# Loading K transposed by DMA in a two-layer decode attention kernel

## Chip, cores and metric

The kernel runs on one core of a Trainium2 chip. The metric is the device time of one execution, in microseconds, and a kernel's time is the median of its runs. The profile used for the reading is that of one more execution of the same program.

## What is computed

Eight batch elements with one token each go through the same attention block and the same small MLP twice. There are 32 query heads, 8 key/value heads (four query heads share one), 8192 cached keys, and heads of 128 elements. Everything in memory is bf16. Both layers read the same K and V caches, which hold 134 MB each.

```python
def _A_ref(x, k_cache, v_cache, wq, wo):
    q = (x @ wq).reshape(B, Sq, Hq, Dh).transpose(0, 2, 1, 3)     # Sq = 1
    k = jnp.repeat(k_cache, rep, axis=1)                         # [B, 8, 8192, 128] -> 32 heads
    v = jnp.repeat(v_cache, rep, axis=1)
    scores = jnp.einsum("bhqd,bhkd->bhqk", q, k) * (Dh ** -0.5)
    p = _softmax(scores, axis=-1)
    o = jnp.einsum("bhqk,bhkd->bhqd", p, v)
    return o.transpose(0, 2, 1, 3).reshape(B, Sq, Hq * Dh) @ wo
...
x = x + _A_ref(_layernorm(x), A_k_cache, A_v_cache, A_wq, A_wo)
x = x + silu(_layernorm(x) @ w1) @ w2
x = x + _A_ref(_layernorm(x), A_k_cache, A_v_cache, A_wq, A_wo)
x = x + silu(_layernorm(x) @ w1) @ w2
```

## The kernel before

**Tasks and steps.** A task is one layer, one batch element and one key/value head: 128 tasks. Its 8192 keys are four granules of 2048 keys, and a granule is two steps of 1024 keys, so a task has eight steps (`GPT`) and the program 1024 positions. `make_tasks` writes the order of tasks out by hand, so that the second layer of one batch element lies among the first layer of the next.

**Loads.** A granule of K or of V is half a megabyte and fills one slot of an arena in SBUF with 27 slots. `plan_loads` works out ahead of time which load goes into which slot and after which position of the program it may be issued. The last 18 granules of K of a batch element (`KEEP`) stay in their slots, transposed, from the first layer to the second. So there are 512 loads of V and 368 of K. All loads are issued by SyncE (SP) into one queue, through `issue` and `dma` (L311), and a load that is to overwrite a slot first waits for the last reader of that slot. A partition p of a slot receives the 16 consecutive rows p*16 to p*16+15 of the granule, 4 KB in one run, so column block c of a slot holds the keys p*16 + c.

**A step.** At position p the loop at the end issues, in this order: the transposes of K for position p + 3 (`emit_t`, `LT` = 3), the scores of position p (`emit_s`), the PV product of position p - 14 (`emit_pv`, `LP` = 14), one piece of the softmax, and, when one is pending, one stage of the chain that follows attention.

- `emit_t` (L408) makes eight PE transposes of 128x128 into a bank of PSUM, and a copy brings the bank back into the same slot: on ScalarE (L414) for three of eight, on VectorE (L416) for the others. It is left out for granules that are kept.
- `emit_s` (L443) makes two matmuls, each with 512 keys as the moving operand. The query stands in a zeroed 128-column window that is shifted by one column for each block of 512 keys, so that 16 blocks and 4 heads fill 64 rows of one PSUM bank.
- The softmax takes a maximum (L452 to L462), an exponential on ScalarE (L466), a sum (L472, L475), and four PE transposes of the probabilities (L484) whose copy is `PT` (L488).
- `emit_pv` (L505) makes eight matmuls: the stationary operand is a 128x128 block of V, and the moving one the four columns of probabilities of that block's keys. These columns lie 16 elements apart in `PT`.
- `emit_norm` (L519) multiplies the four output columns by the reciprocal of the sum.

**The chain.** When a batch element's last first-layer task is done, `chain_of` queues its output projection, layer norm, MLP, second layer norm and second query projection (the matmuls are at L573). One stage is taken at each position, and each stands in PE's program order between the steps of attention, so PE waits there for VectorE's layer norm. The same block for all eight batch elements at once ends the program.

Every engine executes in program order. Waits are semaphore waits that `Sync` derives from who wrote and read each named buffer.

Of the kernel before, what the change touches and what calls it, by code (L numbers as in the profile page):

```python
# [12 lines left out]
GRP = 8  # L13
GPT = 8
GPG = 2
# [8 lines left out]
NQB = 2  # L24
NST = 4
KB = 512
ACT_EVAC = (1, 4, 7)

BF16 = mybir.dt.bfloat16
# [3 lines left out]
ALU = mybir.AluOpType  # L33
# [3 lines left out]
class Tok:  # L37
    __slots__ = ("sem", "val")

    def __init__(self, sem, val):  # L40
        self.sem = sem
        self.val = val
# [78 lines left out]
class Load:  # L121
# [4 lines left out]
    def __init__(self, kind, b, g, k, need, free):  # L126
        self.kind, self.b, self.g, self.k = kind, b, g, k
        self.need, self.free = need, free
        self.slot, self.after = None, None


def make_tasks(nb, nkv, keep_from):
# [57 lines left out]
def _build(ctx, nc, A_x, A_k_cache, A_v_cache, A_wq, A_wo, B_w1, B_w2, out):  # L190
# [4 lines left out]
    REP = HQ // HKV  # L195
# [3 lines left out]
    NGRAN = NCH // (GRP * GPG)  # L199
    SLOT = GRP * GPG * 128  # L200
# [3 lines left out]
    kept = set(order[len(order) - KEEP:])  # L204
# [7 lines left out]
    dve = nc.vector  # L212
    act = nc.scalar
    pool = nc.gpsimd
    sp = nc.sync
# [3 lines left out]
    def sb(shape, dt, name):  # L219
        _cnt[0] += 1  # L220
        return ctx.enter_context(nc.sbuf_tensor(f"{name}_{_cnt[0]}", shape, dt))

    def ps_bank(name, dt=FP32):
        _cnt[0] += 1
        n = 512 if dt == FP32 else 1024
        return ctx.enter_context(nc.psum_tensor(f"{name}_{_cnt[0]}", [128, n], dt))

    ARENA = sb([128, NSLOT * SLOT], BF16, "arena")

    def chunk(slot, c):  # L230
        o = slot * SLOT + c * 128
        return ARENA[:, o:o + 128]

    def half(slot, h):
        o = slot * SLOT + h * GRP * 128
        return ARENA[:, o:o + GRP * 128]
# [6 lines left out]
    XT = [sb([128, KT, B], BF16, f"XT{n}") for n in range(3)]  # L243
    NJ = NCH * 128 // KB
    NR = NJ * REP
    CPB = KB // 128
    JPG = GRP * 128 // KB
    assert NR <= 128 and NJ % 16 == 0 and JPG * KB == GRP * 128
    QT1 = sb([128, B * HQ], BF16, "QT1")
    QT2 = [sb([128, HQ], BF16, "QT2") for _ in range(2)]  # L250
    QB = [sb([128, NJ - 1 + 128], BF16, "QB") for _ in range(NQB)]
# [11 lines left out]
    hsT = sb([128, FT * B], BF16, "hsT")  # L263
    assert KB == D
    P = sb([128, KB], BF16, "P")
    Xr = P
# [8 lines left out]
    rcp = [sb([128, REP], FP32, "rcp") for _ in range(NST)]  # L275

    SCp = [ps_bank("SCp") for _ in range(NSCP)]
    OTp = [ps_bank("OTp") for _ in range(2)]
# [4 lines left out]
    slsem = [DmaCounter(syn.new_sem(f"sl{i}")) for i in range(NSLOT)]  # L283
# [5 lines left out]
    def res(name):  # L289
        if name not in R:  # L290
            R[name] = Res(name)
        return R[name]

    def r_half(slot, h):
        return res(f"slot{slot}_{h}")

    def op(eng, inst_fn, reads=(), writes=()):
        reads = [res(n) if isinstance(n, str) else n for n in reads]
        writes = [res(n) if isinstance(n, str) else n for n in writes]
        syn.acquire(eng, reads, writes)  # L300
        inst = inst_fn()
        tok = syn.mark(inst, eng)
        syn.release(tok, reads, writes)
        return tok

    def dma(eng, out_ap, in_ap, counter, reads=(), writes=()):
        reads = [res(n) if isinstance(n, str) else n for n in reads]
        writes = [res(n) if isinstance(n, str) else n for n in writes]
        syn.acquire(eng, reads, writes)
        tok = counter.next_tok()  # L310
        eng.dma_start(out_ap, in_ap).then_inc(counter.sem, 16)  # L311
        syn.release(tok, reads, writes)
        return tok

    def mm_group(steps, reads=(), writes=()):
        def run():
            inst = None
            for f in steps:
                inst = f()
            return inst  # L320
        return op(pe, run, reads, writes)
# [6 lines left out]

    def issue(d):
        cache = A_k_cache if d.kind == "K" else A_v_cache  # L330
        src = cache[d.b, d.g].rearrange("(k p c) d -> k p (c d)", k=NGRAN, p=128)[d.k]
        dst = ARENA[:, d.slot * SLOT:(d.slot + 1) * SLOT]
        dma(sp, dst, src, slsem[d.slot], writes=[r_half(d.slot, 0), r_half(d.slot, 1)])
        (k_slot if d.kind == "K" else v_slot)[(d.b, d.g, d.k)] = d.slot

    with nc.Block() as block:

        @block.sync
        def _(sync_eng):
            dma(sp, Xr[0:B, :], x_in, wsem["x"], writes=["P"])  # L340

            op(pool, lambda: pool.memset(ident[:, :], 1.0), writes=["ident"])
# [6 lines left out]
                reads=["ident"], writes=["ident"],  # L349
# [5 lines left out]
            for n in range(NST):  # L355
# [5 lines left out]
                reads=["ident"], writes=["hm"],  # L361
# [4 lines left out]
            def issue_until(pos):  # L366
                while queue and queue[0].after <= pos:
                    issue(queue.pop(0))

            def load_wq():  # L370
                src = A_wq.rearrange("(kt p) n -> p kt n", p=128)
                h = KT // 2
                dma(sp, wq_sb[:, 0:h, :], src[:, 0:h, :], wsem["wq"], writes=["wq"])
                dma(sp, wq_sb[:, h:KT, :], src[:, h:KT, :], wsem["wq"], writes=["wq"])
# [6 lines left out]
            for _n in range(NGRAN):  # L381
                issue(queue.pop(0))
# [7 lines left out]

            def has_t(i):
                layer, _b, g = tasks[i // GPT]
                return layer == 0 or (g, (i % GPT) // GPG) not in kept

            def where(i):
                _l, b, g = tasks[i // GPT]
                return b, g, (i % GPT) // GPG, i % GPG

            def emit_t(i):
# [12 lines left out]
                dst = half(slot, h)  # L412
                if n % 8 in ACT_EVAC:
                    op(act, lambda: act.copy(dst, TPp[tb][:, :]), reads=[f"TP{tb}"], writes=[r_half(slot, h)])  # L414
# [3 lines left out]
            def emit_t_until(i):  # L418
                while tnext[0] <= min(i, NG - 1):
                    if has_t(tnext[0]):  # L420
                        emit_t(tnext[0])
                    tnext[0] += 1
# [10 lines left out]
            def emit_s(i):  # L433
                ti = i // GPT
                b, g, k, h = where(i)
                slot = k_slot[(b, g, k)]
                bank, qn = ti % NSCP, ti % NQB
                keys = half(slot, h)
                steps = []
                for c in range(JPG):  # L440
                    j = (i % GPT) * JPG + c
                    steps.append(
                        lambda c=c, j=j: pe.matmul(  # L443
                            SCp[bank][:, :], QB[qn][:, NJ - 1 - j:NJ - 1 - j + 128], keys[:, c * KB:(c + 1) * KB],
                            start=(j == 0), stop=(j == NJ - 1),
                        )
                    )
                mm_group(steps, reads=[r_half(slot, h), f"QB{qn}"], writes=[f"SC{bank}"])
# [45 lines left out]
            def emit_pv(i):  # L494
                ti = i // GPT
                b, g, k, h = where(i)
                slot = v_slot[(b, g, k)]
                ob, pb = ti % 2, ti % NPT
                pv = PT[pb][:, :, :].rearrange("p c (r j) -> p c j r", j=NJ)
                otp = OTp[ob][:, 0:REP]  # L500
                steps = []
                for c in range(GRP):
                    cc = (i % GPT) * GRP + c
                    steps.append(
                        lambda c=c, cc=cc: pe.matmul(  # L505
                            otp, chunk(slot, h * GRP + c), pv[:, cc % CPB, cc // CPB, :],
                            start=(cc == 0), stop=(cc == NCH - 1),
                        )
                    )
                mm_group(steps, reads=[r_half(slot, h), f"PT{pb}"], writes=[f"OT{ob}"])  # L510

            def emit_norm(ti):
                layer, b, g = tasks[ti]
                ob, st = ti % 2, ti % NST
                if layer == 0:
                    dst, rd = at1[b % 2][:, g * REP:(g + 1) * REP], f"at1_{b % 2}"
                else:
                    dst, rd = at2[:, g * REP:(g + 1) * REP, b], "at2"
                op(dve, lambda: dve.tensor_tensor(dst, OTp[ob][:, 0:REP], rcp[st][:, :], ALU.mult),  # L519
                   reads=[f"OT{ob}", f"rcp{st}"], writes=[rd])  # L520

            def ln_stages(xv, rx, n):
# [100 lines left out]
            def chain_of(b):  # L623
# [16 lines left out]
                reads=["P", "ident"], writes=["MISC"],  # L640
            )
            op(dve, lambda: dve.tensor_copy(XT[0][:, :, :], MISC[:, 0:KT * B].rearrange("p (k b) -> p k b", b=B)),
               reads=["MISC"], writes=["XT0"])
# [13 lines left out]
            for p in range(NG + LP + GPT + 1):  # L657
                tq = (p + LQ) // GPT
                if (p + LQ) % GPT == 0 and tq < ntask:
                    layer, b, _g = tasks[tq]  # L660
# [15 lines left out]
                if done >= 0 and done % GPT == 0 and done // GPT < ntask:  # L676
                    tj = done // GPT
                    emit_norm(tj)
                    layer, b, _g = tasks[tj]
# [7 lines left out]
            for f in block_stages(  # L687
# [11 lines left out]
                reads=["XT0", "ident"], writes=["MISC"],  # L699
# [33 lines left out]
```

## Time and profile before

| | |
|---|---|
| Median of 3 runs | 1338.75 us (1329.92 to 1340.53) |
| Profiled execution: time, span | 1341.24 us, 1339.1 us |
| Granted TensorE clock, mean | 0.928 |
| Busy: PE, DVE, ACT, POOL | 1177.7 us (88%), 632.0 us (47%), 391.9 us (29%), 70.9 us (5%) |
| Read from memory | 473.44 MB, 354 GB/s over the span |
| K loads, V loads | 368 and 512, 512 KB each; median 12.8 and 10.1 us from issue to landing |

The span is what the profile's instructions cover; the time has a little around it. Busy time of PE is not PE at its peak, since matmuls overlap: the durations in the timeline overlap too, and what an instruction really occupies is read from start to start. The DMA share in a stretch is the mean busy share of the core's 16 DMA engines; around 1 they are full. The granted clock is given as a share of full speed.

### The profile page before, as it was taken

The numbers are of one execution on the slowest core, as the hardware profiler recorded it, in microseconds if no ns is written. First come the engines' busy times: TensorE is split into PE (matmuls) and PEld (weight loads), VectorE is DVE, ScalarE is ACT, GpSimd is POOL, SyncE is SP. The second block draws the span as 40 slices with busy tenths as digits, with TensorE's granted clock in tenths as the row PEclk, the third lists the DMA queues.
The fourth block names the chain that finished last, engine by engine and source line by source line (L and its number), as shares of the span: only waits on it lengthen the run. The fifth ranks groups of instructions, "written<-read, shape, count | busy, mean of one in ns | idle before, by whom it ended". The sixth has DMA issues, their size and how long they took to land.

```text
span 1339.1 us, 45854 instructions
## 1 busy us (share of the span) xinstructions
PE 1177.7 (88%) x19644; PEld 909.4 (68%) x19960; DVE 632.0 (47%) x1977; ACT 391.9 (29%) x670; POOL 70.9 (5%) x176
## 2 busy tenths in 40 slices
PE   3978799889988899889998889988998889988896
PEld 3656667676767667677676766767776776767665
DVE  2544345544554445545455444554545445445443
ACT  1323123323233223322233222432323222333220
POOL 0000000000000000000000000000000000000000
PEclk7989799989999799998999789997999979999796
DMA  8999599979999699987999779997999959999693
GB/s 348 385 400 405 200 391 407 387 261 399 408 409 357 234 392 408 407 340 275 410 408 405 284 297 402 407 403 272 377 408 407 383 191 383 408 408 372 229 409 154
DMA packets 133944, 476.45 MB, mean 356 GB/s; under 512 B 14176, under 2 KB 20080, under 8 KB 133232
## 3 DMA queue, kind: packets, MB, share of 16 engines
q1 hardware_dynamic: 133744, 473.51, 90.6%
q8 instruction: 159, 2.61, 0.8%
q14 instruction: 41, 0.34, 0.1%
HBM read 473.44 MB, written 0.01 MB: 354 GB/s over the span
## 4 chain that ended last, share of the span: by engine, by line
PE 45%; DMA 41%; DVE 6%; SPq 3%; issue 3%; POOL 0%; ACT 0%; POOLq 0%; DVEq 0%
DMA arena<-in_A_k_cache_dram 40%; PE SCp L443 18%; PE TPp L408 11%; PE OTp L505 8%; PE MISC L573 7%; SPq L311 3%; PE TPp L484 1%; DVE arena L416 1%; DMA wq<-in_A_wq_dram 1%; DVE yr L559 1%; DVE tr L557 1%; DVE tr L556 1%; DVE mxa L452 1%; DVE xnT L561 0%; DVE yr L551 0%
## 5 line engine op out<-in xcount | busy, mean ns | idle before, releaser
L443 PE MATMUL SCp<-arena,QB 128*128 128x512 bf16 x1732 | 561.9, 392 | 24.5 <-PE TPp L408 3.1
L505 PEld LDWEIGHTS OTp<-PT,arena 128*128 128x128 bf16 x8192 | 365.4, 97 | 265.6 <-issue 26.9
L408 PE MATMUL TPp<-ident,arena 128*128 128x128 bf16 x5888 | 474.7, 227 | 72.1 <-DMA arena<-in_A_k_cache_dram 59.8
L416 DVE COPY arena<-TPp 128x1024 bf16<-128x1024 bf16 x460 | 318.1, 692 | 387.1 <-PE TPp L408 386.7
L414 ACT COPY arena<-TPp 128x1024 bf16<-128x1024 bf16 x276 | 279.3, 1012 | 677.6 <-PE TPp L408 677.6
L408 PEld LDWEIGHTS TPp<-ident,arena 128*128 128x128 bf16 x5888 | 356.7, 101 | 98.2 <-DMA arena<-in_A_k_cache_dram 82.6
L505 PE MATMUL OTp<-PT,arena 128*128 128x4 bf16 x8192 | 365.5, 169 | 9.6 <-DMA arena<-in_A_v_cache_dram 8.0
L443 PEld LDWEIGHTS SCp<-arena,QB 128*128 128x128 bf16 x2048 | 153.3, 101 | 7.6 <-PE SCp L443 5.3
L466 ACT ACTIVATE P<-SCp,mxb 64x512 bf16<-64x512 f32 x128 | 87.3, 682 | 178.3 <-DVE mxb L462 175.0
L475 POOL PARTITION_ALL_REDUCE ssa<-ssm x128 | 55.5, 434 | 1065.6 <-DVE ssm L472 1065.6
L452 DVE TENSOR_REDUCE mxa<-SCp 64x1 f32<-64x512 f32 x128 | 85.6, 669 | 29.5 <-PE SCp L443 29.5
L488 DVE COPY PT<-TPp 128x256 bf16<-128x256 bf16 x128 | 37.4, 292 | 109.8 <-PE TPp L484 109.8
L573 PE MATMUL MISC<-xnT,wq 128*128 128x1 bf16 (+1 forms) x1152 | 31.6, 165 | 29.9 <-DVE xnT L561 29.9
L573 PEld LDWEIGHTS MISC<-xnT,wq 128*128 128x128 bf16 x1152 | 30.9, 102 | 30.6 <-DVE xnT L561 25.6
L484 PE MATMUL TPp<-ident,P 128*128 128x128 bf16 x512 | 49.9, 220 | 0.0
L472 DVE TENSOR_SCALAR ssm<-hm,rs 64x4 f32<-64x4 f32 x128 | 27.6, 215 | 36.4 <-ACT P L466 36.4
L431 ACT COPY QB<-QT 128x4 bf16<-128x4 bf16 x128 | 26.2, 206 | 32.6 <-DVE QT L619 32.6
L573 PE MATMUL MISC<-at,wo 128*128 128x1 bf16 (+1 forms) x1152 | 30.9, 164 | 3.5 <-issue 3.2
L573 PEld LDWEIGHTS MISC<-at,wo 128*128 128x128 bf16 x1152 | 30.1, 97 | 3.8 <-issue 3.4
L484 PEld LDWEIGHTS TPp<-ident,P 128*128 128x128 bf16 x512 | 30.3, 97 | 0.3
L519 DVE TENSOR_TENSOR at<-OTp,rcp 128x4 bf16<-128x4 f32 x128 | 21.1, 165 | 15.0 <-PE OTp L505 15.0
L462 DVE STREAM_TRANSPOSE mxb<-mxa 64x32 f32<-64x32 f32 x128 | 26.1, 204 | 4.4
(46 smaller groups left out, 254.9 us busy)
## 6 DMA issues: line engine op xcount, KB each, us to landing
arena<-in_A_v_cache_dram SPq DMA_DIRECT2D x512, 512.0 KB, 10.1
arena<-in_A_k_cache_dram SPq DMA_DIRECT2D x368, 512.0 KB, 12.8
wq<-in_A_wq_dram SPq DMA_DIRECT2D x2, 2048.0 KB, 9.0
wo<-in_A_wo_dram SPq DMA_DIRECT2D x1, 4096.0 KB, 26.1
w<-in_B_w_dram SPq DMA_DIRECT2D x2, 1792.0 KB, 22.6
P<-in_A_x_dram SPq DMA_DIRECT2D x1, 8.0 KB
out_dram<-P SPq DMA_DIRECT2D x1, 8.0 KB
```

Source lines behind the costliest of these rows:

```text
L311: eng.dma_start(out_ap, in_ap).then_inc(counter.sem, 16)
L408: lambda c=c: pe.transpose(tpv[:, c, :], chunk(slot, h * GRP + c), ident[:, :])
L414: op(act, lambda: act.copy(dst, TPp[tb][:, :]), reads=[f"TP{tb}"], writes=[r_half(slot, h)])
L416: op(dve, lambda: dve.tensor_copy(dst, TPp[tb][:, :]), reads=[f"TP{tb}"], writes=[r_half(slot, h)])
L443: lambda c=c, j=j: pe.matmul(SCp[bank][:, :], QB[qn][:, NJ - 1 - j:NJ - 1 - j + 128], keys[:, c * KB:(c + 1) * KB], start=(j == 0), stop=( ...
L452: op(dve, lambda: dve.tensor_reduce(mxa[:, 0:1], SCp[bank][0:NR, :], AX.X, ALU.max), reads=[f"SC{bank}"], writes=["mxa"])
L466: op(act, lambda: act.activation(P[0:NR, :], SCp[bank][0:NR, :], ACT.Exp, bias=mxb[:, 0:1], scale=SM_SCALE, accum_out=rs[st][:, :]), reads ...
L475: op(pool, lambda: pool.partition_all_reduce(ssa[st][:, :], ssm[st][:, :], 128, bass.bass_isa.ReduceOp.add), reads=[f"ssm{st}"], writes=[f ...
L484: lambda c=c: pe.transpose(tpv[:, c, :], P[:, c * 128:(c + 1) * 128], ident[:, :])
L488: op(dve, lambda: dve.tensor_copy(PT[pb][:, :, :], tpv[:, :, 0:NR]), reads=[f"TP{tb}"], writes=[f"PT{pb}"])
L505: lambda c=c, cc=cc: pe.matmul(otp, chunk(slot, h * GRP + c), pv[:, cc % CPB, cc // CPB, :], start=(cc == 0), stop=(cc == NCH - 1),)
L573: lambda o=o, k=k: pe.matmul(MISC[:, o * n:(o + 1) * n], w_sb[:, k, o * 128:(o + 1) * 128], rhs_of(k), start=(k == 0), stop=(k == kparts - 1),
```

## The change

`by_dma` decides which granules of K are loaded by a DMA that transposes; it returns True for all. Such a load writes the 128 elements of a head to the 128 partitions and the granule's 2048 keys, in their order in memory, along a partition. `has_t` is then never true, so `emit_t` issues nothing: 5888 transposes on PE and 736 copies are gone. Since V's rows are still spread as before, the scores of a block must come out in the order of V's blocks: the moving operand of a scores matmul is now four runs of 128 keys, each run stepping through the slot sixteen elements at a time. In PV each of the four moving columns is given eight times (`PVN`), so that a matmul has 32 moving columns and writes 32 columns of PSUM; `emit_norm` reads every eighth. The plan of loads, the slots, and the order on SP stay as they were.

```diff
+PVN = 8
...
+def by_dma(g, k):
+    return True
...
-    def dma(eng, out_ap, in_ap, counter, reads=(), writes=()):
+    def dma(eng, out_ap, in_ap, counter, reads=(), writes=(), turn=False):
...
-        eng.dma_start(out_ap, in_ap).then_inc(counter.sem, 16)
+        if turn:
+            eng.dma_start_transpose(out_ap, in_ap).then_inc(counter.sem, 16)
+        else:
+            eng.dma_start(out_ap, in_ap).then_inc(counter.sem, 16)
...
-        src = cache[d.b, d.g].rearrange("(k p c) d -> k p (c d)", k=NGRAN, p=128)[d.k]
         dst = ARENA[:, d.slot * SLOT:(d.slot + 1) * SLOT]
-        dma(sp, dst, src, slsem[d.slot], writes=[r_half(d.slot, 0), r_half(d.slot, 1)])
+        if d.kind == "K" and by_dma(d.g, d.k):
+            src = cache[d.b, d.g].rearrange("(k n) d -> k n d", k=NGRAN)[d.k]
+            dst = dst.rearrange("p (o n) -> p o n", o=1)
+        else:
+            src = cache[d.b, d.g].rearrange("(k p c) d -> k p (c d)", k=NGRAN, p=128)[d.k]
+        dma(sp, dst, src, slsem[d.slot], writes=[r_half(d.slot, 0), r_half(d.slot, 1)],
+            turn=d.kind == "K" and by_dma(d.g, d.k))
...
             def has_t(i):
                 layer, _b, g = tasks[i // GPT]
-                return layer == 0 or (g, (i % GPT) // GPG) not in kept
+                k = (i % GPT) // GPG
+                return not by_dma(g, k) and (layer == 0 or (g, k) not in kept)
...
-                keys = half(slot, h)
+                if by_dma(g, k):
+                    keys = ARENA[:, slot * SLOT:(slot + 1) * SLOT].rearrange("p (n c) -> p c n", c=GRP * GPG)
+                    keys = keys[:, h * GRP:(h + 1) * GRP, :]
+                else:
+                    keys = half(slot, h).rearrange("p (c n) -> p c n", n=128)
...
-                            SCp[bank][:, :], QB[qn][:, NJ - 1 - j:NJ - 1 - j + 128], keys[:, c * KB:(c + 1) * KB],
+                            SCp[bank][:, :], QB[qn][:, NJ - 1 - j:NJ - 1 - j + 128], keys[:, c * CPB:(c + 1) * CPB, :],
...
-                otp = OTp[ob][:, 0:REP]
+                otp = OTp[ob][:, 0:REP * PVN].rearrange("p (r n) -> p r n", n=PVN)
...
-                            otp, chunk(slot, h * GRP + c), pv[:, cc % CPB, cc // CPB, :],
+                            otp, chunk(slot, h * GRP + c), pv[:, cc % CPB, cc // CPB, :].unsqueeze(2).to_broadcast([128, REP, PVN]),
...
-                op(dve, lambda: dve.tensor_tensor(dst, OTp[ob][:, 0:REP], rcp[st][:, :], ALU.mult),
+                op(dve, lambda: dve.tensor_tensor(dst, OTp[ob][:, 0:REP * PVN:PVN], rcp[st][:, :], ALU.mult),
```

## The prediction

> **What bounds the kernel now.** I read four views in this order: the page with its slices, the stretches between and inside the slow slices, the timeline of single steps, and the DMA view of one short stretch.
>
> The page first: slices of the span with the bandwidth, then the chain, then the costliest groups.
>
> ```profile
> GB/s 348 385 400 405 200 391 407 387 261 399 408 409 357 234 392 408 407 340 275 410 408 405 284 297 402 407 403 272 377 408 407 383 191 383 408 408 372 229 409 154
> ...
> PE 45%; DMA 41%; DVE 6%; SPq 3%; issue 3%; POOL 0%; ACT 0%; POOLq 0%; DVEq 0%
> ...
> L408 PE MATMUL TPp<-ident,arena 128*128 128x128 bf16 x5888 | 474.7, 227 | 72.1 <-DMA arena<-in_A_k_cache_dram 59.8
> L416 DVE COPY arena<-TPp 128x1024 bf16<-128x1024 bf16 x460 | 318.1, 692 | 387.1 <-PE TPp L408 386.7
> L414 ACT COPY arena<-TPp 128x1024 bf16<-128x1024 bf16 x276 | 279.3, 1012 | 677.6 <-PE TPp L408 677.6
> ```
>
> The transposes keep PE busy for 474.7 us and their copies keep two engines busy for 597 us, but most slices stand at 400 to 410 GB/s, and the transposes themselves wait for K to arrive. The plateau never rises above 410: that is the ceiling of the loads. The chain alternates between PE (45%) and DMA (41%), so one share alone does not name the bound. Eight times the rate falls below 300. The next view puts a dip beside the plateau that follows it (columns: width, busy us per engine, granted clock, DMA share, GB/s).
>
> ```profile
> 137.00:168.00 31.00, 22.41 (x532) 19.42 (x535) 12.46 (x57) 4.20 (x7) 2.00 (x5) 0.72 0.49 183
> 168.00:268.00 100.00, 93.09 (x1443) 69.33 (x1470) 49.50 (x144) 32.82 (x58) 5.20 (x12) 1.00 1.01 395
> 268.00:299.00 31.00, 26.87 (x602) 23.06 (x607) 14.78 (x64) 6.92 (x12) 2.46 (x6) 0.84 0.70 260
> ```
>
> On the plateau the DMA engines are full (share 1.01). In a dip, which is the one-token chain of projections and layer norms of a batch element, PE waits in program order for VectorE's norm, slots are not freed, and the loads run dry. Widths times (1 - share) over the eight dips (shares 0.49, 0.70, 0.66, 0.66, 0.60, 0.69, 0.57, 0.53; widths 31 to 36 us) give 101 us without loads.
>
> So the span splits up by DMA. K is 368 loads of 524,288 bytes, 192.9 MB; V is 512, 268.4 MB; weights 12.1 MB. At 409 GB/s V and weights take 686 us, and 688 with the weights' short rows (below); K takes 472, or 1.28 us a load. That is 1160 of 1339 us. The other 179 are the dips (101), the end after the last V load (1314 to 1339, 25), the start (4.5 MB in 16 us, 5 lost), and 48 of small gaps on the plateaus.
>
> Now single steps of PE: two scores matmuls and eight PV matmuls, with and without eight transposes.
>
> ```profile
> 142.87 0.61 PE L408 MATMUL TPp<-ident,arena 128*128 128x128 bf16 x8
> 143.31 0.59 PE L443 MATMUL SCp<-arena,QB 128*128 128x512 bf16 x2
> 143.74 0.36 PE L505 MATMUL OTp<-PT,arena 128*128 128x4 bf16 x8
> 143.96 0.61 PE L408 MATMUL TPp<-ident,arena 128*128 128x128 bf16 x8
> ...
> 656.23 0.61 PE L443 MATMUL SCp<-arena,QB 128*128 128x512 bf16 x2
> 656.67 0.35 PE L505 MATMUL OTp<-PT,arena 128*128 128x4 bf16 x8
> 656.90 0.60 PE L443 MATMUL SCp<-arena,QB 128*128 128x512 bf16 x2
> ```
>
> From start to start: eight transposes 0.44 us (54 ns each), two scores 0.43 (0.215 each), eight PV 0.22 (28 ns each); a step takes 1.09 us with transposes and 0.67 without. Eight steps with transposes and four P transposes are 8.9 us, while the task's 4.2 MB take 10.3 us at 409 GB/s. PE is second already.
>
> **The change, part by part.** *Transposes and copies go.* 736 steps lose 0.43 us of PE, 316 us in all, and DVE and ACT lose 597 us busy. On the plateaus this lies under the loads and is worth nothing; if that cover went, the whole 316 us would count. Inside a dip it is on the path: some ten steps run between the chain's stages, several at half clock (0.87 us for eight transposes), part of it under the norm's waits. I take 6 us a dip.
>
> *PV with 32 columns instead of 4.* Bounds: 28 ns (4 columns) and 54 ns (a transpose moves 128), so 0 to 26 ns times 8192, or 0 to 213 us of PE. I take 0: the one-column projections also go at 25 ns each (128 in 3.20 us), so up to 4 columns the length does not show, and 32 is a quarter of what 54 ns buys. PE has cover: a step of 0.67 is 5.6 us a task, against at least 5.1 us of V and 10.3 of K and V.
>
> *Scores with keys sixteen elements apart.* No long read with such a step is in the trace. Low end 0.215 us, since PV reads PT with the same step and shows nothing with its 4 columns. High end twice that, what the same matmul costs at half clock (two in 0.85 us). I take 0.215. At the high end a step is 1.10 us, today's 1.09: PE's whole saving is gone.
>
> *K by a transposing load.* The number of loads, the slots, the order on SP and the slot waits stay. The scores now wait for the load itself, three steps later than the transposes did, which is slack. What changes is the price of a K load, and nothing in the trace transposes in DMA. Low end: a copy, 1.28 us. For the other end, a row of K is 256 bytes, while the copies of today move 4 KB a partition. The DMA view of the stretch in which wo lands, in 1 KB rows, shows what short packets do:
>
> ```profile
> DMA packets 4003, 4.23 MB, mean 352 GB/s; under 512 B 20, under 2 KB 3961, under 8 KB 4000
> ```
>
> Per engine, 1 KB costs 46.5 ns (352/16 = 22 GB/s), 4 KB costs 160.2 ns (409/16). A line through both has 8.7 ns a packet and 0.037 ns a byte, so 256 bytes cost 18.2 ns: 225 GB/s, 2.33 us a load. Of 1.28 and 2.33 I take a value four fifths of the way up, 2.12 us: the source rows are nearest to the short packets, but wo's rows lie far apart in memory, while a K load is one contiguous half megabyte. A load below 1.28 us I exclude: the plateau at 410 is the ceiling with copies.
>
> The Trainium skill speaks on both sides here. Its page "DMA: Bandwidth & Descriptors", section "Latency and other measured facts", gives a transposing DMA an effective 261 GB/s, measured on one kernel with a non-contiguous middle dimension; "Advanced Engine Details and Errata", section "X-Bar Transpose (TRN2)", calls transposing DMAs as fast as regular ones, 350 to 400 GB/s. By the first this sum would be about 1534 us, by the second 1302 to 1364; no row before the change decides.
>
> *The dips after.* A dip now loses 101/8 = 12.6 us. Six go with the transposes. The nine slots that are not held by kept K (27 - 18) are the loads in flight when PE stalls: 9 x 1.28 = 11.5 us of cover now, 4.5 x (1.28 + 2.12) = 15.3 after, 3.8 more. Left: 2.8 us, 22 in all. With K at the copy's price it is 6.6 each, 53.
>
> *Sum.* 688 + 368 x 2.12 (780) + 78 (end, start, gaps as now) + 22 = 1568 us of span. Around the span the profiled execution has 2 us (1341.24 against 1339.1), and it agrees with the runs' median, 1338.75, within 0.2%. Forecast **1570 us**. Ends: K at 1.28 gives 688 + 472 + 78 + 53 + 2 = 1293; K at 2.33 gives 688 + 857 + 78 + 15 + 2 = 1640. Even is K at about 1.43 us (526 + 47 for the dips): a transposing load may be 12% dearer than a copy before the change loses.
>
> **The rivals.** *A: the transposing load goes at nearly the copy's pace* (below 1.40 us), and the change is faster, 1293 to 1330. For it: a K load reads contiguous memory, and the dips shorten in any case. Against it: a plateau that is already full, and the dearer 1 KB rows. Chance 0.23.
>
> *B: PE becomes the bound through the stepped keys.* At 0.43 us a scores matmul, a task costs 16 x 0.43 + 64 x 0.028 + 0.2 = 8.9 us on all 128 tasks, 1139 us; the eight chains add some 20 us each (10 of projections, 10 of waits), start and end 65: about 1366. It decides if K is cheaper than 1.43 us. Against it: PV's step. Chance 0.07.
>
> *C: transposing loads do not overlap one another.* Today up to nine loads are in flight, and the shortest landing is 3.1 us. If each K load held the queue that long, 688 + 368 x 3.1 + 78 + 2 = 1909. For it: all loads share SP's one queue, so a V load behind a slow K is late too, and then PV and everything behind it on PE. Against it: today's loads overlap. Chance 0.12.
>
> *D: the change does not do what it says*, that is, some K still goes through PE. By_dma returns True for every granule, so I give it nothing.
>
> **How the numbers follow.** The forecast case, K between about 1.45 and 2.4 us, has 0.58 and its own range 1400 to 1650. A makes up nearly all of faster, together 0.22; same, within 1%, gets 0.06 from the edge between A and the forecast; slower, 0.72, is the forecast, B and C. (About 1% is what a measurement of this kernel can tell from no change.) The range reaches from A's end, 1290, to part of C, 1800, and leaves about 2 in 10 out.
>
> **What would show it.** Right: the transposes' and copies' lines gone; K loads land later and the GB/s row stands well below 400 with the DMA share still at 1; scores at 0.215 us and PV at 28 ns start to start; PE's idle time put down to K loads; shallower dips. The clock may fall to 0.5 where PE waits for K, as it does at 72 us today, without costing anything. Wrong: slices with K at 400 GB/s (A); two scores matmuls in 0.86 us at full clock and PE without idle time (B); DMA share below 1 with K in flight (C).

## Result and profile after

The changed kernel takes 2330.64 us (median of 4 runs, 2329.3 to 2333.15), the kernel before 1334.41 (4 runs, with a fresh one beside it). The ratio is 1.747, with a 95% interval of 1.740 to 1.754: slower by three quarters. The profiled execution took 2329.84 us with a span of 2328.1.

From the page of the changed kernel: bandwidth by slice, packets, the chain, and the groups for scores (L461), PV (L523) and the transposes of P (L502).

```profile
GB/s 227 290 244 224 224 238 120 207 229 241 216 124 216 241 234 199 141 209 252 224 187 156 208 261 232 159 172 213 247 240 142 188 207 251 245 126 201 185 249 1
DMA packets 846337, 475.64 MB, mean 204 GB/s; under 512 B 773728, under 2 KB 779632, under 8 KB 845680
...
PE 93%; SPq 4%; DMA 2%; DVE 1%; issue 0%; POOL 0%; POOLq 0%; ACT 0%; DVEq 0%
PE SCp L461 78%; PE OTp L523 9%; PE MISC L591 4%; SPq L317 3%; PE TPp L502 2%; DMA arena<-in_A_v_cache_dram 1%; SPq L319 1%; DMA wq<-in_A_wq_dram 0%; DVE yr L577 0%; DVE tr L575 0%; DVE tr L574 0%; POOL s1a L547 0%; DVE eh L624 0%; POOL s1a L562 0%; DVE XT L601 0%
...
L461 PE MATMUL SCp<-arena,QB 128*128 128x512 bf16 x2048 | 2045.6, 1089 | 2.9 <-ACT QB L445 1.7
...
L523 PE MATMUL OTp<-PT,arena 128*128 128x32 bf16 x8192 | 404.8, 190 | 3.5 <-DMA arena<-in_A_v_cache_dram 2.0
...
L502 PE MATMUL TPp<-ident,P 128*128 128x128 bf16 x512 | 75.3, 301 | 0.0
```

The transposes of K and their copies are gone, as the diff says. The chain is now nearly all PE, and 78% of the span is one line: the scores. Their mean duration went from 392 to 1089 ns, and PE waited only 2.9 us before them, so this is not a wait for K. The mean bandwidth fell from 356 to 204 GB/s, but that is read with care: a second thing has changed in the loads. Packets under 512 bytes went from 14176 to 773728, about one for each of the 368 x 2048 rows of K.

Two stretches of the changed kernel show which of the two decides (last columns: granted clock, DMA share, GB/s; what the clock of 1.00 is worth comes up with PV's columns below):

```profile
880.00:890.00 10.00, 10.00 (x55) 2.71 (x53) 1.98 (x8) 0.77 (x3) 0.00 (x0) 1.00 1.14 251
930.00:940.00 10.00, 10.00 (x55) 2.81 (x53) 1.59 (x6) 0.00 (x0) 0.00 (x0) 1.00 0.40 105
```

PE is busy without a gap in both, once with the DMA engines full and once with them at 0.40. PE sets the pace. One step on the timeline, start to start:

```profile
902.64 2.00 PE L461 MATMUL SCp<-arena,QB 128*128 128x512 bf16 x2
904.45 0.39 PE L523 MATMUL OTp<-PT,arena 128*128 128x32 bf16 x8
904.68 1.99 PE L461 MATMUL SCp<-arena,QB 128*128 128x512 bf16 x2
```

Two scores matmuls take 1.81 us, 0.905 each, against 0.215 before. 2048 x 0.905 is 1853 us. The step is 2.04 us (902.64 to 904.68), against 1.09 before with the transposes in it.

### The profile page after: what moved, and what is told of

It reads as the page before. It is cut to its first block, busy times and chain, and to the rows that moved or that the text cites. A ratio compares the mean times of both kernels' runs of the same rounds, so it can differ in the third digit from the quotient of the medians.

```text
span 2328.1 us, 33179 instructions
## 1 busy us (share of the span) xinstructions
PE 2272.5 (98%) x14072; PEld 652.9 (28%) x14072; DVE 339.2 (15%) x1517; ACT 115.0 (5%) x394; POOL 70.6 (3%) x176
## 2 busy tenths in 40 slices
DMA packets 846337, 475.64 MB, mean 204 GB/s; under 512 B 773728, under 2 KB 779632, under 8 KB 845680
## 3 DMA queue, kind: packets, MB, share of 16 engines
HBM read 280.50 MB, written 0.01 MB: 120 GB/s over the span
## 4 chain that ended last, share of the span: by engine, by line
PE 93%; SPq 4%; DMA 2%; DVE 1%; issue 0%; POOL 0%; POOLq 0%; ACT 0%; DVEq 0%
PE SCp L461 78%; PE OTp L523 9%; PE MISC L591 4%; SPq L317 3%; PE TPp L502 2%; DMA arena<-in_A_v_cache_dram 1%; SPq L319 1%; DMA wq<-in_A_wq_dram 0%; DVE yr L577 0%; DVE tr L575 0%; DVE tr L574 0%; POOL s1a L547 0%; DVE eh L624 0%; POOL s1a L562 0%; DVE XT L601 0%
## 5 line engine op out<-in xcount | busy, mean ns | idle before, releaser
L461 PE MATMUL SCp<-arena,QB 128*128 128x512 bf16 x2048 | 2045.6, 1089 | 2.9 <-ACT QB L445 1.7
L523 PEld LDWEIGHTS OTp<-PT,arena 128*128 128x128 bf16 x8192 | 418.0, 109 | 1593.3 <-issue 1165.8
L523 PE MATMUL OTp<-PT,arena 128*128 128x32 bf16 x8192 | 404.8, 190 | 3.5 <-DMA arena<-in_A_v_cache_dram 2.0
L461 PEld LDWEIGHTS SCp<-arena,QB 128*128 128x128 bf16 x2048 | 152.1, 113 | 29.8 <-issue 15.2
L502 PE MATMUL TPp<-ident,P 128*128 128x128 bf16 x512 | 75.3, 301 | 0.0
L502 PEld LDWEIGHTS TPp<-ident,P 128*128 128x128 bf16 x512 | 44.1, 126 | 1.6 <-issue 1.6
L480 DVE STREAM_TRANSPOSE mxb<-mxa 64x32 f32<-64x32 f32 x128 | 26.1, 204 | 4.4
L472 DVE STREAM_TRANSPOSE mxb<-mxa 64x32 f32<-64x32 f32 x128 | 26.0, 203 | 4.4
L484 ACT ACTIVATION_READ_ACCUMULATOR P<-SCp,mxb 64x1 f32 x128 | 24.2, 189 | 0.0
L473 DVE TENSOR_REDUCE mxh<-mxb 64x2 f32<-64x32 f32 x128 | 22.8, 178 | 4.4
L476 DVE TENSOR_SCALAR mxa<-mxh 64x32 f32<-64x32 f32 x128 | 22.2, 173 | 4.4
```

The source lines that it names most:

```text
L461: lambda c=c, j=j: pe.matmul(SCp[bank][:, :], QB[qn][:, NJ - 1 - j:NJ - 1 - j + 128], keys[:, c * CPB:(c + 1) * CPB, :], start=(j == 0), s ...
L472: op(dve, lambda: dve.transpose(mxb[:, :], mxa[:, :]), reads=["mxa"], writes=["mxb"])
L480: op(dve, lambda: dve.transpose(mxb[:, :], mxa[:, :]), reads=["mxa"], writes=["mxb"])
L484: op(act, lambda: act.activation(P[0:NR, :], SCp[bank][0:NR, :], ACT.Exp, bias=mxb[:, 0:1], scale=SM_SCALE, accum_out=rs[st][:, :]), reads ...
L502: lambda c=c: pe.transpose(tpv[:, c, :], P[:, c * 128:(c + 1) * 128], ident[:, :])
L523: lambda c=c, cc=cc: pe.matmul(otp, chunk(slot, h * GRP + c), pv[:, cc % CPB, cc // CPB, :].unsqueeze(2).to_broadcast([128, REP, PVN]), st ...
```

## The experiments

Theory 1: the scores' read of keys sixteen elements apart binds PE, and under it lies a second bound, a transposing load that costs more than twice a copy. Theory 2: the transposing loads are the cause, and the long matmuls only show PE's wait for them. Each kernel below ran once, except the one of ten runs; thirteen runs of the kernel before beside that one lie between 1327 and 1336 us. The code is shortened: `ARENA[slot]` stands for the slot's part of the arena, and lines that only adapt a shape or an index are left out.

**The transposing load alone** (k_dma_contig).

```diff
-keys = ARENA[slot].rearrange("p (n c) -> p c n", c=GRP * GPG)[:, h * GRP:(h + 1) * GRP, :]
+keys = half(slot, h).rearrange("p (c n) -> p c n", n=128)
```

> K by the transposing load, PV with 32 columns, but the scores read each block of 512 keys as one contiguous run. Left out: the reordering of keys, so probabilities meet other keys' V. Theory 1 (the stepped keys bind PE, 0.91 us a scores matmul): scores fall back to 0.215 us, PE falls far below 98% busy, and the loads set the time. A pair of one K and one V load took 4.2 us on SP in the fullest stretches after the change; less 1.28 for V that is 2.9 a K load, so 688 + 368 x 2.9 + 78 = about 1830 us. With the 2.12 us of the prediction it would be 1570. Theory 2 (PE waits behind the transposing loads, and the long matmuls only show that wait): the time stays above 2200.

Measured: 1832.14 us, span 1830.4. Theory 2 falls: 498 us of the span go with the step alone. What is left is bound by the loads. A stretch of it (clock, DMA share, GB/s at the end), SyncE's queue, and PE's longest wait (total, times, longest):

```profile
740.00:760.00 20.00, 12.38 (x104) 5.03 (x104) 2.20 (x9) 0.87 (x3) 0.65 (x2) 0.50 1.11 245
...
702.24 0.53 SPq L319 DMA_DIRECT2D arena<-in_A_v_cache_dram  x1
702.87 3.51 SPq L317 DMA_TRANSPOSE arena<-in_A_k_cache_dram  x1
706.47 0.53 SPq L319 DMA_DIRECT2D arena<-in_A_v_cache_dram  x1
...
PE OTp L522 <- DMA arena<-in_A_v_cache_dram: 604.8, 330, 24.1
```

PE is idle for more than a third of the stretch, the DMA engines are full, and yet only 245 GB/s arrive. A pair of one K and one V load takes 4.23 us of the queue.

**The stepped read alone** (pe_turn_step16).

```diff
 # kernel before, K copied and transposed on PE
-keys = half(slot, h)
+keys = half(slot, h).rearrange("p (n c) -> p c n", c=16)
...
-keys[:, c * KB:(c + 1) * KB]
+keys[:, c * 8:(c + 1) * 8, :]
```

> The kernel before, K copied and transposed on PE, with one edit: the scores read keys sixteen elements apart within the half granule. Left out: the keys' right order. Theory 1: a scores matmul takes 0.91 us here too; a step is 2.48 us with transposes (736 of them) and 2.05 without (288), 1825 + 590 + 30 for P, and the chains and ends, about 2600 us in all. Theory 2: the step costs nothing and the time stays at 1340.

Measured: 2908.41 us. The step alone, on K loaded as before, more than doubles the time, so theory 1 holds without any transposing load. The expectation was some 300 us short, and the timeline says why:

```profile
699.38 2.00 PE L443 MATMUL SCp<-arena,QB 128*128 128x512 bf16 x2
701.20 0.38 PE L505 MATMUL OTp<-PT,arena 128*128 128x4 bf16 x8
701.43 0.59 PE L484 MATMUL TPp<-ident,P 128*128 128x128 bf16 x4
701.81 2.02 PE L443 MATMUL SCp<-arena,QB 128*128 128x512 bf16 x2
```

Scores cost 0.91 us as assumed, but four transposes take 0.38 us where they took 0.22 before: the run is at half clock (mean granted clock 0.503). 736 groups of K transposes at 0.81 us (median) in place of 0.43 are 280 us more, and P's transposes 20, which makes up the missing 300.

**A transposition that costs nothing** (k_copy).

```diff
 # k_dma_contig, and K by the plain copy of before, not transposed anywhere
-        if d.kind == "K" and by_dma(d.g, d.k):
+        if False:
...
-            turn=d.kind == "K" and by_dma(d.g, d.k))
+            turn=False)
```

> As k_dma_contig, but K comes by the plain copy of before and is transposed nowhere. Left out: the transposition of K. It shows what a transposition that costs nothing would be worth: by the prediction's low end, 688 + 472 + 78 + 53 + 2 = 1293 us. If the dips do not shorten it is 1340; if they were set by the transposes alone it is near 1240.

Measured: 1277.34 us, beside 1334.36 for the kernel before on the same chip: 57 us less. The dip after the first batch element is shallower, 0.61 of the DMA engines against 0.49:

```profile
137.00:168.00 31.00, 23.79 (x466) 16.57 (x463) 11.43 (x60) 2.04 (x7) 2.43 (x6) 0.61 0.61 232
```

So 4% is all that taking the transposes off PE brings while V and K still have to be loaded in this order (this kernel also has PV's 32 columns, worth 5 of the 57 us if they bring here what they bring alone, below). Spread over 368 loads, 57 us are 0.15 us: a transposing load may take 1.43 us, against 1.28 for a copy, before the change loses.

**Short rows without a transposition** (k_copy_256).

```diff
 # k_copy, K in sixteen runs of 256 bytes a partition
-src = cache[d.b, d.g].rearrange("(k p c) d -> k p (c d)", k=NGRAN, p=128)[d.k]
+src = cache[d.b, d.g].rearrange("(k c p) d -> k p c d", k=NGRAN, p=128)[d.k]
```

> As k_copy, but the plain copy of K takes rows of 256 bytes one by one (sixteen per partition, from rows that lie 32 KB apart), as short as the rows that the transposing load reads. Left out: the transposition of K. With the prediction's straight line (8.7 ns a packet and 0.037 ns a byte, 2.33 us a load) it is 688 + 857 + 78 + 15 = 1640 us. If the short rows are the whole price of the transposing load (2.9 us), it is 1830. If the price is that of transposing alone, it stays at 1280.

Measured: 1676.13 us, span 1674.4. The page counts 767840 packets under 512 bytes, nearly as many as with the transposing loads. The span is 398.8 us over k_copy, 1.08 us a load, so a plain load in 256-byte rows costs 2.36 us. The straight line through 1 KB and 4 KB gave 2.33. The transposing load costs (1830.4 - 1275.6) / 368 = 1.51 us more than the copy, 2.79 us, or 188 GB/s. (This is a mean over the run; in the densest stretches a pair takes 4.23 us, which leaves 2.95 for K.) Of that surplus the short rows account for 72% by this comparison, and 0.42 us a load (156 us in all) come on top.

**How the price depends on the step** (step4, step8, step2).

```diff
 # the changed kernel; VR = 4 (8, 2): V in runs of VR rows, keys VR elements apart
-src = cache[d.b, d.g].rearrange("(k p c) d -> k p (c d)", k=NGRAN, p=128)[d.k]
+src = cache[d.b, d.g].rearrange("(k b p c) d -> k p b (c d)", k=NGRAN, p=128, c=VR)[d.k]
...
-keys = ARENA[slot].rearrange("p (n c) -> p c n", c=GRP * GPG)
+keys = ARENA[slot].rearrange("p (b n c) -> p b c n", n=128, c=VR)
```

> The changed kernel with V loaded in runs of four rows (1 KB) in place of sixteen, so that the scores step four elements (8 bytes) in place of sixteen (32 bytes); the same numbers are computed. If the cost of a stepped read grows with the bytes between two elements, a scores matmul takes 0.215 to 0.3 us and the loads set the time: 1830 as above plus 37 for V in short rows, about 1870. If any step at all, or the four separate runs, costs the full price, it is 0.91 us and 2330 again.

Measured: 1909.29 us. The loads bind most of the time, as for a cheap step: PE waits 490 us for V. (The 37 us for V's short rows was a slip: 268.4 MB at 352 in place of 409 GB/s are 106 us, which makes 1940.) The step is not free, though: between 700 and 740 us PE has no idle time. From the timeline of step4, there and (after the dots) in a stretch at a granted clock of 0.50, and below it step2:

```profile
703.64 1.06 PE L463 MATMUL SCp<-arena,QB 128*128 128x512 bf16 x2
704.52 0.37 PE L525 MATMUL OTp<-PT,arena 128*128 128x32 bf16 x8
704.75 0.38 PE L504 MATMUL TPp<-ident,P 128*128 128x128 bf16 x4
704.97 1.06 PE L463 MATMUL SCp<-arena,QB 128*128 128x512 bf16 x2
...
670.09 1.06 PE L463 MATMUL SCp<-arena,QB 128*128 128x512 bf16 x2
670.98 0.40 PE L525 MATMUL OTp<-PT,arena 128*128 128x32 bf16 x8
```

```profile
690.12 0.61 PE L463 MATMUL SCp<-arena,QB 128*128 128x512 bf16 x2
690.58 0.35 PE L525 MATMUL OTp<-PT,arena 128*128 128x32 bf16 x8
```

Two scores take 0.88 us at 8 bytes, 0.44 each, with P's transposes at full clock beside them (0.22 for four). At half clock the two take 0.89. At 4 bytes they take 0.46, hardly more than the 0.43 of a contiguous read.

> As step4, with V in runs of eight rows and scores that step eight elements (16 bytes); the same numbers are computed. Step 1 took 0.215 us a matmul, step 4 0.445, step 16 0.91. If step 8 goes with step 4 the loads set the time, about 1850 us; if it goes with step 16, PE does, 2330; halfway (0.64) a step is 1.5 us and the time stays with the loads or just above, 1850 to 1900.

Measured: 2295.58 us. Scores take 0.89 us each (692.53 - 690.75 = 1.78 for two), and PE binds: 16 bytes cost nearly what 32 do.

> As step4, with V in runs of two rows (512 bytes) and scores that step two elements (4 bytes); the same numbers are computed. The scores should take 0.215 us if two elements 4 bytes apart come in one read, or 0.3 us if the price rises with every step. The loads set the time in either case: V in 512-byte rows is 27.6 ns a packet by the straight line, 1.77 us a load, 250 us more than at 4 KB, so about 2080.

Measured: 1971.9 us, bound by the loads. V in 512-byte rows was overpriced: 140 us over k_dma_contig, 0.27 us a load, where the line gave 0.49.

**PV's columns** (after_pvn1, pe_turn_pvn8).

```diff
 # after_pvn1: the changed kernel
-PVN = 8
+PVN = 1
```

> The changed kernel with PV's columns given once (4 moving columns) in place of eight times. The kernel before with stepped scores ran at a granted clock of 0.50 with 4 columns, the changed kernel at 1.00 with 32. If the columns make the difference, the clock falls to 0.5 here; the stepped scores stay at 0.91 us, as they did at 0.50, and only P's transposes, PV and the projections get longer: some 60 to 120 us more, 2390 to 2450. If the columns do nothing, it is 2330 at a clock of 1.00.

Measured: 2330.35 us, against 2330.64 with eight copies. In the changed kernel the columns do nothing, and my reading of the clock was wrong. The record says 1.00 for both, yet four transposes of P take 0.38 us in them too. From the changed kernel, and below it k_dma_contig in a stretch where the record says 0.50:

```profile
915.14 0.59 PE L502 MATMUL TPp<-ident,P 128*128 128x128 bf16 x4
915.52 2.02 PE L461 MATMUL SCp<-arena,QB 128*128 128x512 bf16 x2
...
748.93 0.59 PE L501 MATMUL TPp<-ident,P 128*128 128x128 bf16 x4
749.31 1.06 PE L460 MATMUL SCp<-arena,QB 128*128 128x512 bf16 x2
```

The durations decide: all three kernels with steps of 16 run at half clock, whatever the number of columns. The pages of the two kernels with a clock of 1.00 have no row of the clock at all, so the 1.00 there is no measurement. Half clock alone does not bind PE: in its stretch at 0.50 (740 to 760 us, above) k_dma_contig leaves PE idle for more than a third.

> The kernel before with PV's columns given eight times, nothing else. If 32 columns take as long as 4 (0.22 us for eight PV matmuls) and do nothing for the clock: within 0.5% of before, 1334. If each costs up to a transpose's 54 ns, PE has 26 ns x 8192 = 213 us more, a step with transposes is 1.30 us, and PE becomes the bound of the plateaus: about 1400. If more columns keep the clock up in the dips: 1300 to 1325.

Measured over ten runs against thirteen: 1326.76 us against 1331.97, ratio 0.9967 (0.9948 to 0.9986). Eight PV matmuls take the same 0.22 us. The gain of 0.3% is too small to call the kernel faster, though its interval leaves out no change. The mean clock is 0.936 to 0.946 over its runs, against 0.928 to 0.936; that the clock brings the gain was not isolated. It is the one version here that, with the full computation, does not lose to the kernel before.

**V from another queue** (v_on_act).

```diff
 # k_dma_contig
-dma(sp, dst, src, slsem[d.slot], ...
+dma(sp if d.kind == "K" else act, dst, src, slsem[d.slot], ...
```

> As k_dma_contig (1830 us), with the V loads issued from ScalarE's queue in place of SyncE's; the K loads stay on SyncE's. Left out: the reordering of keys, as there. SyncE is held some 3.5 us by each transposing load and 0.53 by each V load behind it. If that hold is SyncE's own work, K loads need 368 x 3.5 = 1290 us and V runs beside them: 1450 to 1550 us. If it is back-pressure from DMA engines that are full (share 1.06), the time stays within 2% of 1830.

Measured: 1897.14 us. SyncE's own work would have given 1450 to 1550, so that is not what limits the transposing loads: with V taken off its queue each holds SyncE for 3.7 us (median) in place of 3.5 and lands after 7.6 in place of 5.7, and in a dense stretch (640 to 680 us, DMA share 1.18) the rate is 246 GB/s, as in k_dma_contig. But the time did not stay either. From the waits of this kernel (total, times, longest):

```profile
PE SCp L460 <- DMA arena<-in_A_k_cache_dram: 723.8, 240, 23.5
```

PE now waits for K, up to 23.5 us at once, where in k_dma_contig it waited for V. So V seems to get ahead of K on the shared DMA engines. V's waits for free slots now also stand in ScalarE's program order, and before its copies of the query (QB) ScalarE stands idle for 507 us in all until a PV product ends. Why the sum is 3.5% worse was not isolated.

## Why the prediction was wrong

The spans form a chain, in which each term is the difference of two runs: 1332 before, - 57 for the transposes and PV's columns (k_copy, 1275.6), + 399 for rows of 256 bytes (1674.4), + 156 for transposing in the load (1830.4), + 498 for the stepped scores (2328.1). The forecast of 1570 had both losses, the load and the scores, too small.

- **What bound the kernel, and what the transposes were worth: right.** K at a copy's price gave 1293; k_copy measured 1277. The even point of 1.43 us a K load is also what k_copy gives.
- **PV with 32 columns at no cost: right,** in both kernels that changed it alone (after_pvn1, pe_turn_pvn8).
- **The K load: the direction right, the size too small.** I had the row's own arithmetic at 2.33 us and shaded it to 2.12 because K is contiguous. The plain load in 256-byte rows measured 2.36, and the transposing one 2.79. The contiguous source, for which I shaded it, brought nothing that shows: the packets still carry one row each. And the sum had no term for transposing in itself. With 2.79 it gives 688 + 1027 + 78 + 22 + 2 = 1817; k_dma_contig, from which the 2.79 comes, took 1832. The Trainium skill's 261 GB/s ("DMA: Bandwidth & Descriptors", "Latency and other measured facts") would be, by estimate, 2.0 us a load, and the 350 to 400 of "X-Bar Transpose (TRN2)" in "Advanced Engine Details and Errata" 1.3 to 1.5; the 188 GB/s measured here lies below both.
- **The scores with stepped keys: the step that failed.** I gave 0.215 us and an upper end of 0.43, from the same matmul at half clock. It measured 0.905, and with that PE became the bound: of the 760 us by which the forecast was short, 498 go with the stepped read. Both ends came from rows that could not show it. PV's read with the same step has four columns, and eight PV matmuls take the same 0.22 us with 4 and with 32, so that row shows no length at all. The half clock is another mechanism, not a bound for this one. An operation that the trace doesn't show had got a narrow range and a chance of 0.07, rival B. With the measured prices B's own sum, 16 x 0.905 + 64 x 0.030 + 0.38 = 16.8 us a task, 128 tasks, 160 for the chains and 65 for the ends, comes to 2375. The mechanism stood in the prediction; even its dear end was half of the price. Nor did B need a cheap K: at 16.8 us a task PE lies above the loads even at 2.79, 4 x (2.79 + 1.28) = 16.3 us.
- **Rival C** (transposing loads that do not overlap) is not needed: in k_dma_contig the DMA share is above 1, and a K load lands 5.7 us after its issue (median) while a pair of loads is issued every 4.2, so they overlap.
- **The signs named beforehand** told it at once: B's sign was PE without idle time. Its other sign, two scores in 0.86 us at full clock, did not come: the changed kernel takes 1.81, at half clock. It is step4, with a smaller step, that comes near it (0.88).

## What to carry to other kernels

A change that turns data in the loads is paid twice: in the load, where the row that one packet carries counts, and at the reader, if the new order makes it step through memory. A row of four columns says nothing of the rate at which 512 are read: where no long read with that step is in the trace, the range must be wide. And before a busy engine is relieved, ask what its relief could bring at most: here leaving the transposes out altogether saved 4%.

## What the hardware showed that was not expected

A scores matmul with 512 moving columns costs, start to start, by the distance of two elements in SBUF: 2 bytes 0.215 us, 4 bytes 0.23, 8 bytes 0.44, 16 bytes 0.89, 32 bytes 0.905. From 4 bytes on these are all four runs of 128 keys, and at 4 bytes they cost next to nothing, so it is the distance that costs and not the number of runs; with eight runs of 64 keys at 32 bytes (pe_turn_step16) it is 0.91. At 8 bytes and full clock two matmuls take 0.88 where a contiguous read takes 0.43, so there the read sets the pace and not the array; at half clock they take 0.88 to 0.91, where a contiguous read itself takes 0.81 to 0.86. At 16 and 32 bytes the scores ran at half clock only, so that the price there at full clock stays open: how much of the 0.905 is the step and how much the clock is not known. Open too is why PE, busy without a gap, stayed at half clock (in pe_turn_step16 at 0.50 from 20 us to the end).

The granted clock of the record was 1.00 in kernels whose transposes had the durations of 0.50, so a record is to be held against a known duration. And the count of bytes read from memory, 280.50 MB in the changed kernel, is V and the weights alone: it leaves the transposing loads out.
